# A retention and channel-mix kernel on one core: work placed by a period, attention two blocks ahead, and the decay origin kept for two chunks

## The chip, the cores and the metric

The kernel runs on one core of one Trainium2 chip. The metric is the device time of one execution in microseconds (us), lower is better. The kernel before takes 207.55 us (median of four runs, 206.38 to 208.09). Every run also has the span of its core (first to last instruction, some 1.8 us less than the time) and the mean clock that TensorE was granted. Runs over 1.5% above the fastest of the same kernel are called slow, and comparisons use fast runs.

Names in the profile: PE is TensorE, DVE is VectorE, ACT is ScalarE, POOL is GpSimd. Tiles keep the program's names: `ks` is the scaled k, `pT`/`qkT` the transposed q and k, `pA`/`a2t` the scores and their masked copy, `pS`/`sbd` the state and its scaled copy, `pY`/`xT` the attention result, `dx` the difference of neighbouring tokens, `xk` and `xr` the mixed inputs, `pZ` the keys, `pR` the gate, `pV` the values, `osb` the output.

## The reference

Four sequences of 768 tokens, 8 heads of 64. A decaying state gives the attention result; its output goes through a channel mix.

```python
# attention, per token t and head
state = gamma * state + outer(k[t], v[t])
y[t]  = scale * q[t] @ state
# channel mix on x = y, 512 wide
x_prev = x shifted by one token
xk = mu_k * x + (1 - mu_k) * x_prev
xr = mu_r * x + (1 - mu_r) * x_prev
out = sigmoid(xr @ w_r) * (relu(xk @ w_k) ** 2 @ w_v)
```

## The kernel before

The tokens are cut into 24 chunks of 128 and 12 blocks of two chunks (blocks are counted 0 to 11). The order on every engine is the order in the program. Attention runs one block ahead of the keys. The parts that matter:

```python
    def kscale(c, eng=None):                       # ks: GpSimd, first four on VectorE
        (eng or nc.gpsimd).tensor_tensor(out=KS[c], in0=K32[c], in1=gk..., op=ALU.mult)

    def state(c):
        pS = psa.tile([P, NJ, 2 * D], F32, name="pS", tag="a")
        if not first:                              # carry the state over: one identity matmul
            nc.tensor.matmul(pS, lhsT=ident, rhs=SBD[c - 1], start=True, stop=False, ...)
        ...                                        # plus k^T v of this chunk
        nc.vector.tensor_tensor(out=SBD[c]..., in0=pS..., in1=gs..., op=ALU.mult)

    def shift(m):                                  # all three in one place
        nc.gpsimd.tensor_tensor(out=dx, in0=xcur, in1=xprev, op=ALU.subtract)
        for dst, mu in ((XK[m], muk), (XR[m], mur)):
            for j in range(NJ):
                nc.vector.scalar_tensor_tensor(
                    out=dst[:, j], in0=dx[:, j], scalar=mu[:, j : j + 1], in1=xprev[:, j],
                    op0=ALU.mult, op1=ALU.add)
    # ... cut ...
    for m in range(2, NBLK + 1):                   # steady loop, a = 2*(m+1), p = m-1
        store(p - 1, 1)
        ...                                        # kscale and loads of a+2, a+3
        scores(a); state(a); keys(m, 0)
        scores(a + 1); state(a + 1); keys(m, 1)
        retained(a); keys(m, 2); retained(a + 1); keys(m, 3)
        shift(m + 1)
        transposes(a + 2); gate(p, 0); transposes(a + 3); gate(p, 1)
        values(p, 0); store(p, 0); values(p, 1)
```

Both `xk` and `xr` are four small VectorE instructions, each with two inputs in SBUF (`dx` and `xT`).

## Time and profile before

| before, profiled run (207.57 us, span 205.8, clock 0.965) | us |
|---|---|
| TensorE busy / idle | 164.2 / 41.6 |
| VectorE busy | 132.7 |
| steady period (first key matmul of block 4 at 91.34, of block 9 at 162.09) | 14.15 |
| last matmul ends | 201.87 |

Idle is the span less the busy time. Two views are added here. The first is the busy time in stretches of the span: start:end, length, then busy time and instruction count of PE, PEld, DVE, ACT and POOL, the granted clock, DMA share and GB/s.

```profile
40.00:80.00 40.00, 31.18 (x276) 19.44 (x274) 24.70 (x40) 19.48 (x29) 21.84 (x21) 0.90 0.96 93
80.00:160.00 80.00, 73.02 (x688) 47.58 (x688) 60.89 (x99) 45.01 (x70) 42.08 (x38) 1.00 0.82 113
```

TensorE lacks 8.8 us of 40 in the second stretch and 7.0 of 80 in the steady one, where VectorE has 19 us to spare. The second view is the page's groups of instructions: busy time, mean ns of one, idle time before them and what ended it.

```profile
L196 DVE SCALAR_TENSOR_TENSOR xk<-dx,muk,xT 128x256 f16<-128x256 f32 x48 | 34.1, 768 | 24.6 <-POOL dx L191 24.6
L196 DVE SCALAR_TENSOR_TENSOR xr<-dx,mur,xT 128x256 f16<-128x256 f32 x48 | 20.7, 491 | 0.0
```

The two groups do the same work. `xr` has almost its undisturbed mean, `xk` is 277 ns dearer because two `ks` run on GpSimd beside it. Before them lie 24.6 us in which VectorE waits for `dx`.

### The profile page before, as it was taken

The page shows a single profiled execution, that of the slowest core. Times are in us where ns is not written, and L with a number is a line of the kernel's source. Part 1 is how long each engine was busy: PE and PEld are TensorE (multiplying, and loading weights), DVE is VectorE, ACT ScalarE, POOL GpSimd, SP SyncE. Part 2 cuts the span into 40 slices and gives each one's busy share as a digit, 9 for nine tenths or more (in the row PEclk, how much of TensorE's full clock was granted, in tenths as well). Part 3 has the DMA queues.
Part 4 walks back from the last instruction along what each step waited for, and adds up shares of the span by engine and source line. Part 5 has one row for each costly group of instructions (what it writes and reads, how often), then busy time and mean ns, then how long its engine had stood idle before and what let it go on. Part 6 is the DMA issues. An engine that isn't in the chain of part 4 may idle for free.

```text
span 205.8 us, 3572 instructions
## 1 busy us (share of the span) xinstructions
PE 164.2 (80%) x1444; PEld 104.3 (51%) x1444; DVE 132.7 (64%) x232; ACT 95.2 (46%) x146; POOL 90.4 (44%) x88
## 2 busy tenths in 40 slices
PE   0483952798376997997979979979979899899992
PEld 0351731463253745756647447457456475666540
DVE  1485456705598299497596794994985966837021
ACT  2110750295032743825925727438359257282820
POOL 7928205960468391580860933915907003030000
PEclk9999998599968899999999999999999999999999
DMA  7999999994048939379099097393790200202022
GB/s 91 179 194 158 205 184 131 136 151 74 0 102 140 118 25 207 78 50 245 15 81 228 0 147 162 23 200 87 48 243 20 94 8 3 104 0 81 24 102 102
DMA packets 82320, 21.82 MB, mean 106 GB/s; under 512 B 76544, under 2 KB 79232, under 8 KB 82304
## 3 DMA queue, kind: packets, MB, share of 16 engines
q0 software_dynamic: 52544, 8.92, 55.5%
q1 hardware_dynamic: 28704, 12.67, 24.3%
q8 instruction: 11, 0.18, 0.4%
q10 hardware_dynamic: 1056, 0.00, 0.3%
q14 instruction: 5, 0.04, 0.1%
HBM read 24.21 MB, written 6.29 MB: 148 GB/s over the span
## 4 chain that ended last, share of the span: by engine, by line
PE 55%; DVE 25%; issue 7%; POOL 5%; ACT 3%; DMA 3%; POOLq 0%; DVEq 0%
PE pZ L208 17%; PE pV L231 15%; PE pR L221 9%; DVE a2t L140 6%; DVE xr L196 6%; DVE osb L240 5%; PE pY L176 4%; DVE sbd L158 3%; DMA q<-in_q_dram 3%; POOL dx L191 3%; DVE xk L196 3%; PE pS L149 2%; PE pT L123 2%; PE pT L125 2%; PE pY L170 2%
## 5 line engine op out<-in xcount | busy, mean ns | idle before, releaser
L213 ACT ACTIVATE kr<-pZ 128x512 f32<-128x512 f32 x48 | 28.5, 595 | 81.9 <-PE pZ L208 81.8
L191 POOL TENSOR_TENSOR dx<-xT 128x1024 f32<-128x1024 f32 x12 | 22.7, 1888 | 91.1 <-DVE xT L182 91.1
L208 PE MATMUL pZ<-xk,wk 128*128 128x256 f16 x384 | 55.4, 294 | 8.6 <-DVE xk L196 8.5
L196 DVE SCALAR_TENSOR_TENSOR xk<-dx,muk,xT 128x256 f16<-128x256 f32 x48 | 34.1, 768 | 24.6 <-POOL dx L191 24.6
L208 PEld LDWEIGHTS <-wk 128*128 128x128 f16 x384 | 37.9, 104 | 18.5 <-issue 10.5
L231 PE MATMUL pV<-wv,k 128*128 128x512 f16 x192 | 43.6, 379 | 0.0
L140 DVE TENSOR_TENSOR a2t<-pA,c_sb 128x512 f16<-128x512 f32 x48 | 30.7, 679 | 9.4 <-PE pA L134 9.4
L127 ACT COPY qkT<-pT 128x1024 f16<-128x1024 f16 x24 | 24.0, 1008 | 15.3 <-PE pT L125 15.3
L214 ACT ACTIVATE k<-kr 128x512 f16<-128x512 f32 x48 | 30.2, 630 | 1.5
L231 PEld LDWEIGHTS <-k 128*128 128x128 f16 x192 | 18.7, 98 | 22.2
L240 DVE SCALAR_TENSOR_TENSOR osb<-pV,rsb 128x512 f32<-128x512 f32 x24 | 15.7, 682 | 18.8 <-PE pV L231 12.4
L182 DVE TENSOR_TENSOR xT<-pY,gy_sb 128x512 f32<-128x512 f32 x24 | 16.4, 689 | 12.1 <-PE pY L176 11.8
L221 PE MATMUL pR<-wr,xr 128*128 128x512 f16 x96 | 24.0, 379 | 0.0
L116 POOL TENSOR_TENSOR ks<-k,csm_sb 128x512 f16<-128x512 f32 x20 | 22.3, 1131 | 2.0 <-PE pS L153 1.8
L110 POOL DMA_DIRECT2D q<-in_q_dram x24 | 22.3, 929 | 0.8 <-POOLq L379 0.8
L112 POOL DMA_DIRECT2D v<-in_v_dram x24 | 21.8, 908 | 0.0
L196 DVE SCALAR_TENSOR_TENSOR xr<-dx,mur,xT 128x256 f16<-128x256 f32 x48 | 20.7, 491 | 0.0
L134 PE MATMUL pA<-qkT 64*128 64x128 f16 x192 | 12.2, 229 | 7.6 <-DVE a2t L140 5.1
L158 DVE TENSOR_TENSOR sbd<-pS,csm_sb 128x512 f16<-128x512 f32 x24 | 16.3, 679 | 0.0
L123 PE MATMUL pT<-c_sb,q 128*128 128x128 f16 x96 | 9.7, 226 | 8.2 <-DMA q<-in_q_dram 8.2
L226 ACT ACTIVATE rsb<-pR 128x512 f32<-128x512 f32 x24 | 14.3, 604 | 3.3 <-PE pR L221 3.3
L134 PEld LDWEIGHTS <-qkT 64*128 64x128 f16 x192 | 6.5, 98 | 16.2 <-issue 12.5
(25 smaller groups left out, 101.7 us busy)
## 6 DMA issues: line engine op xcount, KB each, us to landing
k<-in_k_dram SPq DMA_DIRECT2D x24, 256.0 KB, 5.2
out_dram<-osb SPq DMA_DIRECT2D x24, 256.0 KB, 3.2
q<-in_q_dram POOLq DMA_DIRECT2D x24, 128.0 KB, 4.6
v<-in_v_dram POOLq DMA_DIRECT2D x24, 128.0 KB, 5.9
wk<-in_moe_w_k_dram POOLq DMA_DIRECT2D x2, 512.0 KB, 9.4
wv<-in_moe_w_v_dram POOLq DMA_DIRECT2D x1, 1024.0 KB, 19.9
wr<-in_moe_w_r_dram POOLq DMA_DIRECT2D x1, 512.0 KB, 14.4
c_sb<-c SPq DMA_DIRECT2D x1, 64.0 KB, 3.2
```

The source lines that it names most:

```text
L110: nc.gpsimd.dma_start(out=Q16[c], in_=q[b, :, t, :].rearrange("h t d -> t h d"))
L127: nc.scalar.copy(out=QKT[c], in_=pT)
L140: nc.vector.tensor_tensor(out=A2[c][:, hp], in0=pA[hp], in1=causal[:, None, :].to_broadcast([P, NJ, C]), op=ALU.mult,)
L158: nc.vector.tensor_tensor(out=SBD[c].rearrange("p j (h d) -> p j h d", h=2), in0=pS.rearrange("p j (h d) -> p j h d", h=2), in1=gs[:, :, : ...
L191: nc.gpsimd.tensor_tensor(out=dx, in0=xcur, in1=xprev, op=ALU.subtract)
L196: nc.vector.scalar_tensor_tensor(out=dst[:, j], in0=dx[:, j], scalar=mu[:, j : j + 1], in1=xprev[:, j], op0=ALU.mult, op1=ALU.add,)
L208: nc.tensor.matmul(pZ[:, i, :], lhsT=wk16[:, co, fo * P : fo * P + P], rhs=XK[m][:, co, :], start=(i == 0 and co == 0), stop=(co == NCO - ...
L213: nc.scalar.activation(out=kr, in_=pZ, func=AF.Relu)
L214: nc.scalar.activation(out=K2[m][:, 2 * g : 2 * g + 2], in_=kr, func=AF.Square)
L221: nc.tensor.matmul(pR, lhsT=XR[m][:, co, tb * P : tb * P + P], rhs=wr16[:, co, :], start=(co == 0), stop=(co == NCO - 1),)
L231: nc.tensor.matmul(pV, lhsT=K2[m][:, fo, tb * P : tb * P + P], rhs=wv16[:, fo, :], start=(fo == 0), stop=(fo == NFO - 1),)
L240: nc.vector.scalar_tensor_tensor(out=osb, in0=PV.pop((m, tb)), scalar=1.0 / (KSC * KSC), in1=RS.pop((m, tb)), op0=ALU.mult, op1=ALU.mult,)
```

## The change

The intent is to place every engine's work at a stated time in a period of 12 us, so that no wait of VectorE is left in front of TensorE. Attention moves from one block ahead to two. `dx` goes between other VectorE work, `xk` and `xr` are parted, and `xr` stands where `dx` of the next block runs. The decay's origin is kept for a pair of chunks, so one PSUM bank holds the state of both and the identity matmul is needed for even chunks only. The last chunk of a sequence makes no state. The first four blocks get places of their own. The core of the diff, shortened and with some lines joined:

```diff
+ORDER = {
+    "att": {
+        "scale": (-5.73, -4.03),
+        "T": (0.1, 2.32),
...
+        "dx": (13.61,),
+        "xk": (14.87,),
+        "xr": (24.22,),
+    },
... ("mix", "load")
+    "start": {0: (-7.04, -3.15, -2.4, -0.25), 1: (-6.26, -2.28, -0.66, 0.5), ...},
+}
-    gk_np = gam[None, :] ** (-ar[:, None])
+    gk_np = np.concatenate([gam[None, :] ** (C - ar[:, None]), gam[None, :] ** (-ar[:, None])], axis=1)
-    outp = pool("outp", 3)
+    outp = pool("outp", 5)
     def state(c):
-        pS = psa.tile([P, NJ, 2 * D], F32, name="pS", tag="a")
-        if not first:
-            nc.tensor.matmul(pS, lhsT=ident, rhs=SBD[c - 1], ...)
+        if even:
+            PSS[c] = psa.tile([P, NJ, 2 * D], F32, name="pS", tag="a")
+            if not first:
+                nc.tensor.matmul(PSS[c], lhsT=ident, rhs=SBD[c - 1], ...)
+        else:
+            PSS[c] = PSS[c - 1]
... (the steady loop is replaced by a plan of times)
+    def attention(n, t0, w=1.0):
+        start = n < 2
+        for i, c in enumerate((2 * n, 2 * n + 1)):
+            last = c % NCH == NCH - 1
+            o = lambda name: t0 + w * EV[name][i]
+            at(o("scale"), scale_k, c, nc.vector if start else nc.gpsimd)
+            if c + 2 < NC:
+                at(o("scale") + 0.01, load_k, c + 2)
...
+            if not last:
+                at(o("S"), state, c)
+                at(o("SE"), kept, c)
...
+        at(t0 + w * EV["dx"][0], differ, n, nc.vector if start else nc.gpsimd)
+        at(t0 + w * EV["xk"][0], mixed, n, XK, muk, "xk16")
+        at(t0 + w * EV["xr"][0], mixed, n, XR, mur, "xr16")
+    for n in range(NBLK):
+        pa, pg, pr, pv = ORDER["start"].get(n, (n - 2, n, n, n))
+        attention(n, pa * T, 0.7 if n < 2 else 1.0)
+        mix_keys(n, pg * T); mix_gate(n, pr * T); mix_values(n, pv * T)
+    for _, _, fn, args in sorted(plan, key=lambda p: p[:2]):
+        fn(*args)
```

## The prediction

> **What bounds the kernel now.** I read the engine shares and the slices first, then the chain of work that ended last in order of time, then TensorE's waits, then the timelines of VectorE and GpSimd for one block, and last the queues of the first 20 us. The page:
>
> ```profile
> PE 164.2 (80%) x1444; PEld 104.3 (51%) x1444; DVE 132.7 (64%) x232; ACT 95.2 (46%) x146; POOL 90.4 (44%) x88
> PE   0483952798376997997979979979979899899992
> PEclk9999998599968899999999999999999999999999
> ```
>
> TensorE has holes in the first twelve slices (to 62 us) and one hole in nearly every later group of three slices. The later holes have a period. The chain over one block of 256 tokens:
>
> ```profile
> 133.66 1.20 DVE osb L240 x2
> 134.86 1.20 DVE a2t L140 x2
> 136.06 0.61 DVE sbd L158
> 136.71 0.38 PE pS L149
> ...
> 143.90 2.83 PE pV L231 x14
> 146.72 1.19 DVE xr L196 x3
> 147.91 1.20 DVE osb L240 x2
> ```
>
> The same link returns after 147.91 - 133.66 = 14.25 us; from 62.0 to 175.2 us eight blocks pass, 14.15 us each. So from xr to sbd VectorE alone carries the chain for about 4.6 us of a block. TensorE's own list of waits says the same:
>
> ```profile
> PE pS L149 <- DVE sbd L158: 8.5, 11, 0.8
> PE pZ L208 <- DVE xk L196: 8.5, 3, 4.4
> PE pA L134 <- DVE a2t L140: 5.1, 8, 1.2
> ```
>
> Most of the pS and pA waits (0.8 us and 0.7 us a block) are the steady hole. The pZ waits are the start: the first blocks do attention, shift and keys one after the other.
>
> What TensorE itself needs I take from the end of the chain, where it runs without a pause: 32 key matmuls in 3.49 us, 8 gate matmuls in 1.73, 16 value matmuls in 3.45, so 8.67 us a block. For a chunk, steps from start to start give transposes 0.45, scores 0.33, carried state 0.23 plus 0.22, result 0.22 plus 0.35: 1.80, or 3.59 for two. A block is 12.26 us and waits about 1.9 us of its 14.15. Twelve blocks are 147.1, less 4 x 0.44 for the four sequences' first chunks: 145.3 us of the 205.8.
>
> Why VectorE is late is seen in the timeline:
>
> ```profile
> 114.60 3.23 DVE L196 SCALAR_TENSOR_TENSOR xk<-dx,muk,xT 128x256 f16<-128x256 f32 x4 [2.07 <-POOL dx L191]
> 114.54 2.22 POOL L116 TENSOR_TENSOR ks<-k,csm_sb 128x512 f16<-128x512 f32 x2
> 184.66 1.67 DVE L196 SCALAR_TENSOR_TENSOR xk<-dx,muk,xT 128x256 f16<-128x256 f32 x4 [2.07 <-POOL dx L191]
> ```
>
> It waits 2.07 us for dx, and its four xk then take 3.23 us beside two ks on GpSimd, against 1.67 us without them.
>
> **What the Trainium skill says.** "SBUF — State Buffer", section "SBUF: two separate sides", calls the port pair of VectorE and GpSimd an exclusive lock, also for a VectorE operation with two SBUF inputs against a GpSimd operation that reads SBUF. The trace agrees: 3.23 against 1.67. Operations with one input in PSUM keep their time beside GpSimd (osb 0.68 at 61.94 us beside a ks). "DMA: Bandwidth & Descriptors", section "Queues, rings and completion order", says that each DMA engine goes round its queues packet by packet. The trace agrees: from 11 to 12 us the two queues moved 159 and 160 packets while their bytes differed (0.15 and 0.04 MB). "TensorE: Matmul & The Clock Gate", "Part 1: The HAM clock gate", says that TensorE runs at half rate until it has been busy for some 3.4 us. The trace agrees roughly: the first keys took 6.50 us for 32, the last 3.49.
>
> **The change, part by part.** *Removed.* The state lives on in one PSUM bank for two chunks, so the identity matmul stands only before even chunks, and a sequence's last chunk keeps no state. The instruction lists give 28 matmuls fewer: 12 identity at 0.22 (2.6 us) and 4 x 4 state matmuls (0.9 us), 3.5 us of TensorE; 145.3 - 3.5 = 141.8. VectorE loses four sbd, 2.4 us in all. *Added.* The decay table is built twice (14 small steps for 7, some 1.9 us before the first ks), and the first two dx go to VectorE, an estimated 1.2 us each from 0.6 for half the size.
>
> *The steady order.* On TensorE a period is now: Z0, Z1, last value half of the block before, T, Z2, S, Z3, T, A, R, V, R, S, A, V, Y, V, Y. It sums to 12.26 - 0.22 = 12.04. I laid the other engines beside it by hand, from the waits built into the instructions. ScalarE needs 4 x 1.23 + 2 x 1.0 + 2 x 0.6 = 8.1 us and delivers each copy 1 to 2 us ahead of its reader. VectorE needs ten operations at 0.60 and eight at 0.39, 9.2 us. xr meets dx on GpSimd (1.89), and xk may meet a ks (1.1), so up to 1.4 + 0.9 more: 10.6 to 11.5 of 12.04. xk is wanted half a period after it is made, and dx lies beside xr and osb instead of in front of a waiting VectorE. The tightest links are sbd before the odd chunk's S, about 0.5 us to spare, and a2t before Y, about 0.9. So nothing but TensorE sets the period, and I allow 0.25 us of slips: 12.3 for 14.15.
>
> *The start.* Here I expect no gain at first. k has two buffers, so k2 is issued only after ks0, which the longer table moves from 6.1 to about 8.1 us. All eight q and v loads of four chunks and both halves of wk stand on the other queue. Before, k2 took 10.2 us from issue and k3 11.2. With the packets shared one to one I estimate k2 at about 18 us, k3 at about 22. In the new order of VectorE ks2 stands ahead of the masking of chunk 1, and ks3 ahead of the second xT, so VectorE waits from about 13 to 18 and again to 22. Then xT 23.2, sbd 23.8, dx 25, xk 27, the second block's attention interleaved until 31, keys 0 from 31 to 37 at the slow clock. Keys 1 starts at about 38.5, before it was 36.4. From there the new order wins: attention of block 2 lies inside keys 1, four gate groups cover the way from xT over dx to xk, and keys 2 starts at about 48.2. By then it has done chunks 0 to 5 (9.45 us), keys 0 and 1 (6.98), four gates (3.46) and half a value group (0.86), 20.75 us; the kernel before is there some 4.5 us of work behind.
>
> *Sum.* 48.2 + (141.8 - 20.75) + 5 of waits until the period holds (q, v and k of block 3 are loaded only after dx of block 2, and land 4 to 5 us later) + 7 x 0.25 slips = 176.0; after the last matmul 3.9 us of osb and store as before (201.9 to 205.8): a span of 180. The reported time was 1.8 us over the span (207.57 against 205.8), so 182 us. Of the 26 us, 3.5 are removed work, about 14 the steady holes, the rest the stretch from 37 to 62 us.
>
> **The rivals.** *VectorE becomes the bound.* For it: 10.6 to 11.5 us of 12.04, and an order in which one late xr moves sbd and a2t. Against it: in the period before VectorE was as busy (32.91 us in three blocks, 11.0 each, with 1.6 us of lock time) and its idle was only in front of dx. If its slips reach TensorE, the period is 12.8 to 13 and the time about 188. *The start's k loads come sooner.* If ks2 and ks3 do not wait, keys 0 starts near 24 and everything comes 6 to 8 us earlier, 175. For it: the order looks tuned and puts ks2 there on purpose. Against it: the 10.2 and 11.2 us that k2 and k3 took. *Nothing gained, because another wait replaces the old one* (pS held over two chunks takes one of four banks, values wait for wv): about 200. Against it: the scores' second pair needs only the first pair's masks, made 0.4 us or more ahead, and wv, which landed at 30.5, has four more transfers of 0.9 us ahead of it, so it lands by 36 to 40 us, used at 48.
>
> **Range and chances.** The start is worth 7 us either way, the steady slips 5 up and 1 down, so 175 to 190. Faster by over 2% means under 203.6 us. Even both bad rivals together stay under that, which leaves a misread order or bank: 0.96 faster, 0.03 within 2%, 0.01 slower.
>
> **What will show it.** Right: a period near 12.3 us in the chain, with TensorE nearly alone on it; pS and pA waits on VectorE almost gone; xr slowed beside dx; VectorE waiting for the DMA of k at ks2 and ks3; TensorE clock full from about 37 us. Wrong: a period of 13 with a2t or sbd in the chain; ks2 without a wait; long TensorE waits for q or v loads at 50 to 60 us.

## The result, and the profile after

The changed kernel took 188.18 us (median of four runs, 186.40 to 189.96) against 207.55. Two runs were fast (187.10 and 186.40, clock 0.999), two slow (189.96 and 189.26, clock 0.99). The ratio of fast runs is 0.9005, 95% interval 0.8932 to 0.9077. A ratio is here always the mean time of one kernel's fast runs over that of the other's in the same rounds, so it is not quite the ratio of the medians quoted, which are of all runs, slow ones too. Run again as a control (e5 below), the same kernel had a median of 186.85 us and a ratio of 0.8951. The result is inside the predicted range and 5 to 6 us over the predicted 182. The profiled run was fast. Its page:

```profile
PE 156.7 (85%) x1416; PEld 101.5 (55%) x1416; DVE 149.7 (81%) x237; ACT 94.3 (51%) x146; POOL 88.1 (48%) x87
PE   0374069899699999999899899899799899999991
```

The span fell by 20.5 us: TensorE's busy time fell by 7.5, its idle time from 41.6 to 28.6, by 13.0. Of the 7.5 us only 3.5 are removed work. Most of the rest is the clock: in the kernel before it is recorded at 0.50 from 34.30 to 41.12, from 58.19 to 61.60 and from 65.02 to 68.43 us. TensorE is busy for 10.2 us of these stretches, so about 5 us are lost there (an estimate: half of the busy time). The changed kernel's profiled run has no such stretch between 31.24 us, where its clock records begin, and the last matmul. All runs of the kernel before have a mean clock of 0.934 to 0.967, the fast ones of the changed kernel 0.996 to 1.000; what keeps the clock up was not tested. VectorE's busy time rose by 17.0 us, although it has four `sbd` less and only two `dx` and a few short operations more. TensorE's slices still have a small dip every third or fourth place. The stretches:

```profile
40.00:80.00 40.00, 37.49 (x343) 23.15 (x341) 31.88 (x49) 23.84 (x36) 30.46 (x30) 1.00 1.18 130
80.00:160.00 80.00, 75.43 (x709) 48.79 (x708) 77.60 (x109) 45.36 (x72) 37.85 (x34) 1.00 0.78 108
96.70:110.40 13.70, 12.80 (x125) 8.39 (x121) 13.25 (x18) 7.60 (x12) 7.49 (x7) 1.00 0.92 115
```

From 40 to 80 us TensorE now lacks 2.5 us instead of 8.8, at a mean clock of 1.00 instead of 0.90. In the steady stretch it still lacks 4.6, and VectorE, which had 19 us to spare, is busy for 77.6 of 80 us. The third line is one period, 13.7 us long, with VectorE busy for 13.25. Its chain of waits in order of time (start, length, what):

```profile
96.77 1.33 PE pZ L282 x12
98.10 4.95 DVE xr L272 x4
103.05 0.60 DVE osb L322
103.65 2.13 DVE xk L272 x4
105.78 0.60 DVE sbd L225
106.38 0.61 DVE a2t L196
...
110.49 1.33 PE pZ L282 x12
111.82 4.95 DVE xr L272 x4
```

This answers to the chain of before. VectorE carries it without a gap from 98.10 to 106.99, 8.9 of 13.7 us, and 4.95 of those are four `xr` whose undisturbed time is 1.66. The waits of TensorE (total us, times, longest) have shrunk, but they are still VectorE's:

```profile
PE pS L216 <- DVE sbd L225: 5.0, 5, 1.8
PE pZ L282 <- DVE xk L272: 2.3, 3, 0.9
```

What the 4.95 us consist of is seen only instruction by instruction. VectorE's timeline (start, length, what):

```profile
98.02 1.81 DVE L272 SCALAR_TENSOR_TENSOR xr<-dx,mur,xT 128x256 f16<-128x256 f32 x1
99.75 1.26 DVE L272 SCALAR_TENSOR_TENSOR xr<-dx,mur,xT 128x256 f16<-128x256 f32 x1
100.94 1.72 DVE L272 SCALAR_TENSOR_TENSOR xr<-dx,mur,xT 128x256 f16<-128x256 f32 x1
102.58 0.47 DVE L272 SCALAR_TENSOR_TENSOR xr<-dx,mur,xT 128x256 f16<-128x256 f32 x1
```

And GpSimd's timeline beside it:

```profile
97.66 1.88 POOL L266 TENSOR_TENSOR dx<-xT 128x1024 f32<-128x1024 f32 x1 [5.56 <-DVE xT L252]
99.50 0.91 POOL L160 DMA_DIRECT2D q<-in_q_dram  x1
100.41 0.88 POOL L165 DMA_DIRECT2D v<-in_v_dram  x1
101.30 1.06 POOL L169 TENSOR_TENSOR ks<-k,csm_sb 128x512 f16<-128x512 f32 x1
```

The fourth `xr` is free: 0.47 us. The first is 1.34 longer, beside `dx`. The second is 0.79 longer although GpSimd shows only the issuing of a load at that time, and the third 1.25 longer, over the end of the issuing and the start of `ks`. Together that is 3.4 us, all of it recorded as busy time of VectorE. In the page's groups the mean of an `xr` rose from 491 to 944 ns, while `xk` fell from 768 to 657.

Counted over all 96 `xk` and `xr`, the time over 0.47 us each sums to 14.9 us before, all in 19 instructions beside a `ks`; 50 instructions beside the issuing of loads were free. After the change it is 31.5 us: 10.3 in seven beside `dx`, 6.6 in nine beside `ks`, 5.8 in eight beside load issues (one of them touches 0.2 us of a `ks`), 8.8 in six that touch both an issue and a `ks` for longer. Not every place before a `ks` stalls: of 22 `xk` and `xr` that began during an issue with a `ks` next or next but one in GpSimd's order, 13 were stalled, and nine, all beside a q issue with the `ks` next, ran free, the fourth `xr` above among them. The 16.6 us between the two sums are nearly all of the 17.0 us by which VectorE's busy time rose.

The start waits where the prediction had said, only shorter. VectorE's timeline of the third and fourth `ks`:

```profile
14.90 0.69 DVE L169 TENSOR_TENSOR ks<-k,csm_sb 128x512 f16<-128x512 f32 x1 [2.48 <-DMA k<-in_k_dram]
20.75 0.69 DVE L169 TENSOR_TENSOR ks<-k,csm_sb 128x512 f16<-128x512 f32 x1 [3.36 <-DMA k<-in_k_dram]
```

The first key matmul of a block, from the traces, is the yardstick for all that follows (profiled runs, us from the span's start; e6 and e11 are experiments):

| | block 0 | 1 | 2 | 4 | 9 | 11 | span |
|---|---|---|---|---|---|---|---|
| before | 18.76 | 36.41 | 60.11 | 91.34 | 162.09 | 187.85 | 205.8 |
| predicted | 31 | 38.5 | 48.2 | | | | 180 |
| after | 30.31 | 36.68 | 46.42 | 82.99 | 150.70 | 171.61 | 185.3 |
| e6 | 29.46 | 36.21 | 45.81 | 82.38 | 144.70 | 165.61 | 179.3 |
| e11 | 25.26 | 32.51 | 44.12 | 78.56 | 140.93 | 161.84 | 175.5 |

The mean period from block 4 to block 9 is 14.15 us before and (150.70 - 82.99) / 5 = 13.54 after. So the steady periods, where the largest gain was expected, give 0.6 us each. After block 9 the changed kernel has no attention left and saves 9.2 us to the last matmul (39.8 to 30.6), of which a block's attention, some 3.6 us, was merely done earlier.

### The profile page after: what moved, and what is told of

It is laid out like the page before. It is cut to its first block, busy times and chain, and to the rows that moved or that the text cites. A ratio compares the mean times of both kernels' runs of the same rounds, so it can differ in the third digit from the quotient of the medians.

```text
span 185.3 us, 3522 instructions
## 1 busy us (share of the span) xinstructions
PE 156.7 (85%) x1416; PEld 101.5 (55%) x1416; DVE 149.7 (81%) x237; ACT 94.3 (51%) x146; POOL 88.1 (48%) x87
## 4 chain that ended last, share of the span: by engine, by line
PE 45%; DVE 37%; DMA 10%; ACT 2%; POOL 2%; issue 1%; SPq 1%; DVEq 0%
PE pV L313 15%; PE pZ L282 15%; DVE xr L272 14%; DVE xk L272 12%; DMA k<-in_k_dram 10%; PE pY L242 4%; PE pR L298 4%; DVE osb L322 3%; PE pA L188 3%; DVE a2t L196 3%; PE pY L236 3%; DVE sbd L225 2%; POOL dx L266 2%; DVE xT L252 2%; ACT k L293 1%
## 5 line engine op out<-in xcount | busy, mean ns | idle before, releaser
L282 PE MATMUL pZ<-xk,wk 128*128 128x256 f16 x384 | 47.8, 274 | 2.3 <-DVE xk L272 2.3
L313 PE MATMUL pV<-wv,k 128*128 128x512 f16 x192 | 49.0, 380 | 0.2 <-DVE osb L322 0.2
L266 POOL TENSOR_TENSOR dx<-xT 128x1024 f32<-128x1024 f32 x10 | 19.2, 1918 | 60.0 <-DVE xT L252 60.0
L272 DVE SCALAR_TENSOR_TENSOR xr<-dx,mur,xT 128x256 f16<-128x256 f32 x48 | 42.5, 944 | 0.0
L282 PEld LDWEIGHTS <-wk 128*128 128x128 f16 x384 | 36.4, 98 | 9.3 <-issue 3.0
L272 DVE SCALAR_TENSOR_TENSOR xk<-dx,muk,xT 128x256 f16<-128x256 f32 x48 | 28.8, 657 | 2.9 <-POOL dx L266 2.8
L313 PEld LDWEIGHTS <-k 128*128 128x128 f16 x192 | 16.9, 98 | 17.5 <-issue 0.8
L177 PE MATMUL pT<-c_sb,q 128*128 128x128 f16 x96 | 10.2, 234 | 7.6 <-DMA q<-in_q_dram 7.6
L225 DVE TENSOR_TENSOR sbd<-pS,csm_sb 128x512 f16<-128x512 f32 x20 | 13.6, 681 | 3.1 <-PE pS L216 3.1
L298 PEld LDWEIGHTS <-xr 128*128 128x128 f16 x96 | 8.7, 98 | 10.0 <-DVE xr L272 0.6
L177 PEld LDWEIGHTS <-q 128*128 128x128 f16 x96 | 7.5, 104 | 10.3 <-DMA q<-in_q_dram 7.9
```

The costliest lines, as they stand in the source:

```text
L266: eng.tensor_tensor(out=DX[m], in0=xcur, in1=xprev, op=ALU.subtract)
L272: nc.vector.scalar_tensor_tensor(out=dst[m][:, j], in0=DX[m][:, j], scalar=mu[:, j : j + 1], in1=xprev[:, j], op0=ALU.mult, op1=ALU.add,)
L282: nc.tensor.matmul(pZ[:, i, :], lhsT=wk16[:, co, fo * P : fo * P + P], rhs=XK[m][:, co, :], start=(i == 0 and co == 0), stop=(co == NCO - ...
L298: nc.tensor.matmul(pR, lhsT=XR[m][:, co, tb * P : tb * P + P], rhs=wr16[:, co, :], start=(co == 0), stop=(co == NCO - 1),)
L313: nc.tensor.matmul(PV[m, tb], lhsT=K2[m][:, fo, tb * P : tb * P + P], rhs=wv16[:, fo, :], start=(fo == 0), stop=(fo == NFO - 1),)
```

## The experiments

The theory: in a period VectorE is late because `xr` stands beside GpSimd's `dx` and `ks` and stalls; without the stall, TensorE alone sets the period at about 12.2 us. The rivals: VectorE simply has too much work; the pairing of chunks cost something; the start, bound by k loads, holds everything back. Three calls were made, each on one chip with its own runs of the kernel before (medians 207.62, 208.11, 206.97). The medians below are of all runs, the ratios of fast runs alone. All kernels gave correct results but e8, which is wrong. All diffs are against the changed kernel.

| run | median us | ratio to before, 95% interval |
|---|---|---|
| e5_after_again | 186.85 | 0.8951 (0.8884 to 0.9018) |
| e1_xr_early | 183.16 | 0.8829 (0.8776 to 0.8883) |
| e2_ks_late | 187.46 | none, three of four runs slow |
| e3_k_early | 185.86 | 0.8928 (0.8885 to 0.8972) |
| e4_no_pair | 188.60 | 0.9092 (0.9036 to 0.9147) |
| e6_xr_from_block_5 | 181.06 | 0.8669 (0.8600 to 0.8738) |
| e7_both | 181.06 | 0.8677 (0.8598 to 0.8755) |
| e8_no_ks | 179.85 | none, one run |
| e9_dx_on_vector | 180.67 | 0.8701 (0.8658 to 0.8743) |
| e10_xr5_dx_start | 181.57 | 0.8746 (0.8697 to 0.8794) |
| e11_best | 177.19 | 0.8580 (0.8540 to 0.8620) |

### e1: xr earlier, where GpSimd does nothing

```diff
-        at(t0 + w * EV["xr"][0], mixed, n, XR, mur, "xr16")
+        at(t0 + w * (EV["xr"][0] if start else 20.8), mixed, n, XR, mur, "xr16")
```

> From the third block on, the four xr stand on VectorE ahead of the two xT of their block, at a time when GpSimd has nothing to do, instead of right behind them, where dx runs; nothing else moves. Theory (VectorE sets the steady period of 13.5 us because its four xr take 5.0 us instead of 1.67 beside dx and what follows it on GpSimd): xr falls to about 1.7 us a block, the period to 12.1 to 12.4 us, where TensorE sets it, and the time falls by 7 to 10 us, to 178 to 180. Rival (TensorE's own order or waits on ScalarE or PSUM banks set the period, and a busy VectorE only fills it): the period stays within 0.3 us of 13.5 and the time within 2 us of the changed kernel.

183.16 us (182.41 to 184.81), some 3 us short of the expected 178 to 180. The mean `xr` fell from 944 to 525 ns, the stalls from 31.5 to 17.9 us in sum, and the periods from block 4 on are 12.62, 12.45, 12.23, 12.01, 13.01 and 12.23 us. No instruction was added or taken away, only `xr` moved. So the steady loss is the place of `xr`. But block 4 began at 84.96, 2.0 us later than in the changed kernel (in this profiled run the clock was 0.953), so the early place seemed a bad one in the first blocks. That led to e6. Only half of it can be: block 1 is already 1.2 us late (37.84 against 36.68), before any moved `xr`. From block 3 to block 4 it is 18.91 us against 17.97, and e6, which leaves these blocks alone, has 17.97 again.

### e2: ks later, xr left where it is

```diff
-            o = lambda name: t0 + w * EV[name][i]
+            o = lambda name: t0 + w * ((-0.9, -0.8) if name == "scale" and n > 2 else EV[name])[i]
```

> From the fourth block on, GpSimd runs dx, then the four issues of q and v loads, then the two ks; in the changed kernel it is dx, q, v, ks, q, ks, v. Theory A (the issue of a q or v load on GpSimd, right after dx, holds up a VectorE operation with two SBUF inputs as a ks does): the four xr still take 4.2 us or more a block, the period stays 13.2 to 13.7, the time within 2 us of the changed kernel. Theory B (only dx and ks hold them up, and the issues do not): one xr waits 1.3 us for dx and the others run freely, 3.0 us for the four, the period is about 12.4 and the time 5 to 8 us less.

Three of four runs were slow (clock 0.981 to 0.991, 187.38 to 187.97), the one fast run took 182.57. The profile, of a slow run, still tells something of VectorE. `xr` falls to 2.99 us: 1.81 beside `dx` and three free ones. Now `xk` pays. VectorE's timeline:

```profile
100.70 2.99 DVE L272 SCALAR_TENSOR_TENSOR xr<-dx,mur,xT 128x256 f16<-128x256 f32 x4
104.21 4.07 DVE L272 SCALAR_TENSOR_TENSOR xk<-dx,muk,xT 128x256 f16<-128x256 f32 x4
```

GpSimd's timeline of the same stretch:

```profile
104.82 0.91 POOL L165 DMA_DIRECT2D v<-in_v_dram  x1
105.71 2.28 POOL L169 TENSOR_TENSOR ks<-k,csm_sb 128x512 f16<-128x512 f32 x2
```

`xr` was free beside issues that stand in front of other issues; `xk` was slowed from 104.21 on, beside the issues that stand in front of the two `ks`, the first of which is recorded at 105.71. The stall went to another instruction: in this run the mean period from block 4 to block 9 is 13.07 us, not the 12.4 of theory B. Whether an issue stalls VectorE by itself or only with a `ks` behind it was left to e8.

### e3: the k loads earlier

```diff
-    ldk = pool("ldk", 2)
+    ldk = pool("ldk", 4)
-            if c + 2 < NC:
-                at(o("scale") + 0.01, load_k, c + 2)
+            if c + 4 < NC:
+                at(o("scale") + 0.01, load_k, c + 4)
+    at(t, load_k, 2)          # right after load_k 1
+    at(t, load_k, 3)
```

> k has four buffers and k2 and k3 are asked for right behind k1, so they no longer wait for ks0 and ks1. Theory (the start is set by k2 and k3, for which VectorE waits 2.5 and 3.4 us with everything behind it): both waits go, the first key matmul comes at 24 to 26 us instead of 30.3, and the time falls by 4 to 6 us. Rival (the queues are full all the time, so what k gains the q, v and wk loads lose): the first key matmul comes at 29 us or later and the time falls by less than 1.5 us.

185.86 us, fast runs 184.60 to 186.08, against 186.15 to 187.41 for the control. The profiled run fell in the slow state, so only the order of its events is used: block 0 began at 24.81 instead of 30.31, 5.5 us sooner, block 2 at 45.02, 1.4 sooner, block 3 no sooner (65.28 against 65.02). The transposes of chunk 4 then waited 1.88 us for their q. The k loads do hold back the first keys, but alone little of that reaches the time: the expected 4 to 6 us were missed. Where it is lost this run cannot tell, for its clock is at 0.50 from 34.24 to 37.65 and from 47.89 to 51.30 us; in e7, a fast run, it is kept up to block 3 and lost before block 4.

### e4: the state without pairs

```diff
-        if even:
+        if True:                       # new bank and identity matmul for every chunk
...
-        else:
-            PSS[c] = PSS[c - 1]
# and the three decay tables as in the kernel before
```

> The decay origin is one chunk again, as in the kernel before: a carried state and an identity matmul for every chunk (12 more identity matmuls of 0.22 us on TensorE, 2.6 us in all); the number of VectorE operations and all places stay. Theory (VectorE sets the steady period): nearly all of it lies beside VectorE's work, and the time rises by 0 to 1.2 us. Rival (TensorE sets the period): it rises by 2.3 to 3 us.

188.60 us (187.90 to 190.23), some 1.8 us over the control, or 2.9 by the ratios (0.9092 against 0.8951). It was run at another time. By the time alone the rival (2.3 to 3 us) is as near as the theory (0 to 1.2), so the periods have to tell. The periods from block 4 on are 13.71, 13.73, 13.14, 13.44, 13.68, 12.23, and those of the changed kernel 13.71, 13.72, 13.15, 13.44, 13.69, 12.23. So the identity matmul that pairing saves is worth nothing while VectorE sets the period: it fills a hole of TensorE. The difference arises between blocks 2 (46.49 against 46.42) and 4 (85.23 against 82.99), where the profile has the granted clock at 0.50 from 49.46 to 52.87 us; why is left open.

### e5: the changed kernel again

> The changed kernel once more, for comparison on the same chip in the same minutes. It was 187.1 and 186.4 us in its fast runs and 189.3 and 190.0 at a granted clock of 0.99; every theory expects 186 to 190.

186.85 us (five fast runs 186.15 to 187.41, one slow 189.49). It is the control for e6 to e8.

### e6: xr earlier from block 4 on only

```diff
-        at(t0 + w * EV["xr"][0], mixed, n, XR, mur, "xr16")
+        at(t0 + w * (EV["xr"][0] if n < 4 else 20.8), mixed, n, XR, mur, "xr16")
```

> As the first experiment (the four xr ahead of their block's two xT on VectorE), but only from the fifth block on, so that the start keeps its order. Theory (the steady period was set by VectorE's stalls beside dx; what the first experiment lost, some 2 us, it lost in the third and fourth block, whose xr had been moved too): the fifth block's keys start within 0.7 us of the changed kernel's 83.0, the period is 12.2 to 12.4, and the time is 6 to 8 us below the changed kernel, 179 to 181. Rival (the 2 us came from a late k load in that run, and moving xr for the third and fourth block costs nothing): no better than the first experiment's 182.4 to 184.8.

181.06 us, 5.8 less than the control. Up to block 4 the two are alike (82.38 against 82.99); then the periods are 12.62, 12.45, 12.22, 12.01, 13.01, 12.23. Busy time in two of these periods:

```profile
107.40:119.70 12.30, 12.30 (x124) 8.03 (x119) 11.29 (x19) 7.59 (x12) 7.49 (x7) 1.00 1.02 131
119.70:131.70 12.00, 12.00 (x119) 7.91 (x117) 10.40 (x17) 7.60 (x12) 7.50 (x7) 1.00 1.01 133
```

TensorE is busy for the whole of both, and only TensorE stands on the chain from 105.98 to 133.01 us. VectorE, with 17 to 19 instructions where the changed kernel's period had 18, is busy for 10.4 to 11.3 us instead of 13.25.

### e7: e6 and e3 together

> xr as in the run before, and four k buffers with k2 and k3 asked for at once as in the third experiment. Theory (the start is bound by the full DMA queues, so early k moves the first keys by 5 us but the third block's only by about 1.4): 1 to 2 us below the run before, 177.5 to 180. Rival (VectorE's stalls hid the early start, and now all 5 us come through): 174 to 176.

181.06 us, the same as e6: the edits of both, and no gain from the second. Neither expectation (177.5 to 180, 174 to 176) was met. At block 3 e7 was 3.9 us ahead (60.51 against 64.41), at block 4 only 0.65 (81.73 against 82.38). TensorE's timeline (the bracket is the idle time before, and what ended it):

```profile
61.86 0.27 PE L282 MATMUL pZ<-xk,wk 128*128 128x256 f16 x1 [0.91 <-DVE xk L272]
63.05 4.99 PE L282 MATMUL pZ<-xk,wk 128*128 128x256 f16 x29 [0.91 <-DVE xk L272]
```

The keys of block 3 twice wait for a stalled `xk`, and then 29 of them take 4.99 us where the end of the kernel before did 32 in 3.49; the granted clock is at 0.50 from 63.72 to 67.13 us, all of it busy, which costs about 1.7 us (half of it, an estimate). So the longer waits and the clock together take back the 3.2 us. The early start brings TensorE to a place where the same stall of VectorE is uncovered; that the clock fell because of these waits is not shown.

### e8: no ks after chunk 7 (wrong on purpose)

```diff
+        if c >= 8:
+            KS[c] = KS[6 + c % 2]      # old data: the result is wrong
+            return
-            if c + 2 < NC:             # and no k loads for those chunks
+            if c + 2 < 8:
```

> Wrong on purpose: from the ninth chunk on ks is not computed and k not loaded (the ks of the seventh and eighth chunk are used again), so in the steady blocks GpSimd has dx and four load issues alone; nothing else moves. Which operation holds up VectorE when the trace shows only a load issue on GpSimd? Theory A (the issues themselves): stalls of about 0.8 us beside issues stay, and the four xr take 3.7 us or more. Theory B (a ks that the record shows later, or dx): no stall beside an issue is left, and the four xr take 3.0 us, one stall of 1.3 us for dx.

One run, 179.85 us, relative error 1.04. With no `ks` left on GpSimd, from block 4 on no `xk` or `xr` stalls beside a load issue any more; the only stall there is the one beside `dx`. VectorE's timeline:

```profile
95.29 3.00 DVE L275 SCALAR_TENSOR_TENSOR xr<-dx,mur,xT 128x256 f16<-128x256 f32 x4
98.81 1.66 DVE L275 SCALAR_TENSOR_TENSOR xk<-dx,muk,xT 128x256 f16<-128x256 f32 x4
```

GpSimd's timeline, with an issue over the whole of that `xk`:

```profile
98.54 0.90 POOL L160 DMA_DIRECT2D q<-in_q_dram  x1
99.41 0.91 POOL L165 DMA_DIRECT2D v<-in_v_dram  x1
```

So it is not the issuing of a load that stalls VectorE. It needs a `ks` behind it, though the free `xr` of above shows that this alone is not enough; what decides stays open. (The edit drops the k loads too. That these were the cause is unlikely: they ran in the kernel before, where all 50 instructions beside issues were free.) The periods are 12.0 to 12.5 us with `dx` still beside `xr`: without the `ks` part, the stall of 1.34 us is covered.

### e9: every dx on VectorE

```diff
-        at(t0 + w * EV["dx"][0], differ, n, nc.vector if start else nc.gpsimd)
+        at(t0 + w * EV["dx"][0], differ, n, nc.vector)
```

> The changed kernel with all twelve dx on VectorE (1.22 us each) instead of the last ten on GpSimd; order and places as they were. VectorE gets 1.2 us more work a block, and GpSimd's 1.9 us of dx is gone. Theory (not VectorE's work but its stalls on what GpSimd runs beside it set the 13.5 us): its work is 10 x 0.60 + 8 x 0.40 + 1.2 = 10.4 us a block, stalls only from the two ks are left, 0 to 1.8 us, so the period is 12.2 to 12.6 and the time 178 to 182. Rival (VectorE is simply out of time): 1.2 us more on it makes the period 13.5 or longer, and the time is 186 or more.

180.67 us. VectorE has 1.2 us of work more in each block, and the kernel is some 6 us faster. Busy time of one period:

```profile
107.10:119.30 12.20, 12.20 (x121) 8.01 (x117) 10.96 (x19) 7.60 (x12) 6.23 (x7) 1.00 1.02 130
```

VectorE's busy time fell from 13.25 of 13.7 to 10.96 of 12.2 although a `dx` of 1.21 us was added. This settles the rival "too much work on VectorE": the bound was the stall. The stalls sum to 9.1 us, the least of all runs.

### e10: e6, and dx of blocks 2 and 3 on VectorE

```diff
-        at(t0 + w * EV["dx"][0], differ, n, nc.vector if start else nc.gpsimd)
+        at(t0 + w * EV["dx"][0], differ, n, nc.vector if n < 4 else nc.gpsimd)
```

> The sixth run's kernel (xr early from the fifth block on), and dx of the third and fourth block on VectorE too, as those of the first two are. Theory (there xk takes 4.0 and 2.5 us behind dx because GpSimd's loads and ks follow dx at once; with dx on VectorE the loads and ks of these blocks run earlier): the two waits of TensorE for xk in those blocks go, the fifth block's keys come 2 to 4 us earlier, and the time is 177 to 179.5. Rival (TensorE has other work to catch up there): under 1 us gained.

181.57 us, two of six runs slow at clock 0.991, the fast ones mostly 180.2 to 180.6. Block 4 began at 81.80, 0.6 us before e6. The expectation of the theory is missed and that of the rival holds: freeing VectorE alone is worth little there.

### e11: e10 and the early k loads together

> The run before with four k buffers and k2 and k3 asked for at once. In the seventh run that gained 3.9 us up to the fourth block and lost it there, where TensorE waited for a stalled xk and its clock dropped. Theory: with that wait gone most of the 3.9 us come through, 174 to 176.5. Rival (the start is bound by the loads): within 1 us of the run before.

177.19 us (176.93 to 178.97), the fastest of all, and 3.3 us under the median of e10's four fast runs (180.52) on the same chip. Block 0 begins at 25.26 and block 4 at 78.56, 3.2 us before e10: what the early loads gain is now kept. From e7 it differs only by the two `dx`: at block 3 the two are alike (61.02 and 60.51), at block 4 e11 is 3.2 us ahead (78.56 and 81.73). It stays some 0.7 us outside what was expected of it. Against the changed kernel it takes 177.19 instead of 186.85 us (ratios to before 0.858 and 0.8951), by another place for `xr`, two `dx` on another engine, earlier k loads and two more k buffers.

## Why the prediction was right or wrong

**Right: what bounds, and the size of the gain.** 182 was predicted, 175 to 190 as the range; 188.18 and 186.85 were measured. That TensorE's holes come from a late VectorE, and that the new order would leave about 12.2 us of TensorE in a period, is shown by e6 and e9: 12.0 to 12.45 us in most of their periods, TensorE busy throughout. The kernel with `xr` placed elsewhere (e6) takes 181.06 us, near the sum.

**Wrong: "xr meets dx on GpSimd (1.89), and xk may meet a ks (1.1), so up to 1.4 + 0.9 more".** This is the term that was mis-sized. For `dx` the 1.4 was good: 1.33 to 1.65. But `xr` also meets the `ks` that GpSimd has queued behind its load issues, which costs another 0.79 and 1.25 us. In place of 1.4 the four `xr` take 3.4 us more than undisturbed, and `xk` some 0.5 in place of 0.9. So `sbd` comes about 2.0 - 0.4 = 1.6 us later than planned, and the tightest link had "about 0.5 us to spare": 1.1 us a period. Measured with and without it, the mean periods from block 4 to block 9 are 13.54 (changed kernel) and 12.46 us (e6), 1.08 apart; with e9 (12.41) and e8 (12.23) it is 1.1 to 1.3. That it fits so closely is in part luck, since each of these three has some stall left. That `xr` would be slowed was foreseen; that a queued `ks` slows it before its own record begins was not to be seen in the kernel before, where the `ks` stood ahead of the issues and 50 of 50 instructions beside issues were free.

**The rival that came true.** "VectorE becomes the bound ... the period is 12.8 to 13 and the time about 188." It was set aside because VectorE had been as busy in the period before, with 1.6 us of lock time. That took the stalls of the old order for those of the new one, where they are 3.4 us for `xr` and 0.5 for `xk`; e9 shows that it is the stalls and not the work that bind: more work, less busy time. The period came out longer still (13.54); that the time is about 188 or less all the same is because the start came sooner than predicted.

**The steady holes, "about 14".** In the five periods from block 4 to block 9 only 5 x (14.15 - 13.54) = 3.0 us came back. The rest of the 20.5 us lies before block 4 (8.35 us, of which some 5 are the half clock of the kernel before, which the prediction's account of the gain does not name) and after block 9 (9.2 us). Of the signs the clock and the k waits were right, while TensorE's waits for `sbd` became fewer, not "almost gone", and the chain has `a2t` and `sbd` in it, which was named as the sign of being wrong.

**The start, right in kind and 1.8 us too slow.** VectorE did wait for the DMA at `ks` 2 and 3, which start at 14.90 and 20.75 us instead of 18 and 22. The keys of blocks 0, 1 and 2 began 0.7, 1.8 and 1.8 us before the estimates. "Keys 0 from 31 to 37 at the slow clock" was wrong: they took 4.11 us. From start to start the first five came some 0.2 us apart and from the sixth on it was 0.11; the trace's first clock record, of a full clock, begins at 31.24 us (what the page shows before that is no measurement). In the kernel before, 24 of the 32 came 0.16 us apart or more, most of them 0.21, and the first record begins at 24.06. E3 and e11 show that the rival of early k loads was worth 5 us at block 0, 1 to 1.5 us of the time when done alone, and about 3.3 when VectorE was freed too; not the 6 to 8 that the prediction gave it.

**Removed work.** The identity matmuls were counted as gain in full. E4 shows that in the steady periods as they came out they are worth nothing. Where TensorE alone is the chain, as in e6, each stands on it with its 0.22 us.

**A smaller miss on TensorE.** The prediction has 12.04 us of TensorE for a full period. In e6, where nothing else is on the chain, it is 12.45, then 12.22 for the block that makes no last state and 12.01 for the one that begins a sequence. On its chain the value and gate groups take 0.86 us in some places, as the prediction counts them (half of 1.73 or a quarter of 3.45), but 0.97 in others, the value groups in front of a result group among them. One period of 13.01 in e1 and e6, between blocks 8 and 9, has `xT`, `dx` (1.90) and an `xk` of 4.38 us for its 1.67 on the chain: there the stall still reaches TensorE.

**Sum.** The last matmul came at 181.31 instead of 176.0. The start is 1.8 us sooner. In the sum a block carries 141.8 / 12 + 0.25 = 12.07 us; the five periods from block 4 to block 9 exceed that by 5 x (13.54 - 12.07) = 7.3, of which 5 x (13.54 - 12.46) = 5.4 is the stall and 2.0 the smaller miss with the odd 13.01. The rest is -0.2. The tail after the last matmul (4.0) and the difference of time to span (1.8) were as predicted.

**Not tested.** The new order as a whole cannot be taken apart from its parts, so what attention two blocks ahead is worth by itself was not measured; nor were the dropped last states, the halved wv load and the deeper output pool. Why some runs of one kernel have a clock of 0.98 to 0.99 and take 2 to 3 us more stays open. The kept traces show what such a mean stands for: a stretch of 3.41 us at 0.50, as in e4 and e7, takes half of 3.41 / 187, some 0.009, off it.

## What to carry to other kernels

Where VectorE has operations with two inputs in SBUF, place them where GpSimd has neither a tensor operation running nor one queued behind its load issues, or try the GpSimd operation on VectorE even if that adds work (e9). A busy share does not tell work from stall: compare the mean time of one instruction with its undisturbed time, one by one, before an engine is called full. An earlier start is only kept if the stage that comes after it is not itself stalled, so test the two together.

## What the Trainium skill lacked or had wrong

- "SBUF — State Buffer", section "SBUF: two separate sides": the traces agree with the exclusive lock (an `xr` of 0.47 us takes 1.81 beside `dx`, an `xk` in the kernel before 1.26 beside a `ks`). It lacks that a stall can show while the trace has GpSimd at issuing loads: seven such stalls of 0.8 us and one of 0.3 in the changed kernel, none once no `ks` follows (e8), none of 50 where the `ks` stands ahead of the issues (before). A reader who looks for the overlap of two records misses them.
- "Perfetto Trace Analysis", sections "GPSIMD Engine Instruction" and "DMA Instruction — SWDGE (GPSIMD)": the first says that a GpSimd instruction's span in a profile is unreliable, the second that two of its processors write the descriptors. The first also says that each of the eight processors keeps its own queue. That the others take up the queued `ks` meanwhile would follow from that and fit the stalls beside issues; no run here shows it, and the page does not draw it out. What it lacks is a warning that such a queued operation can cost another engine time: 5.8 us in eight instructions here.
- No page has what a single meeting costs. Here a `ks` recorded at 1.06 us costs one VectorE instruction about 0.8 us, and a `dx` of 1.88 to 2.00 costs 1.33 to 1.65.
